# A planned first block and a squared relu: one shared port in the plan, a shift convolution summed in PSUM, and a relu that stays in its PSUM bank

## The chip, the cores and the metric

The kernel runs on one core of a Trainium2 chip. The metric is the device time of one execution in microseconds; the time given for a kernel is the median of its runs.

The engines carry the profile's names: PE multiplies matrices (PEld is its weight load), DVE and POOL work on vectors, ACT applies functions and copies, SP issues the DMAs. Each takes its own instructions strictly in order.

## The reference

Two layers, each a gated convolution (A) and a feed-forward net (B), on 2048 tokens of 1024 channels, in float32:

```python
def A(n, k, v, shift_k, ssm_k, ssm_D):       # n: layer norm of x
    k_shift = sum(k_pad[:, t:t + S] * shift_k[:, 3 - t] for t in range(4))
    kv = k_shift * v
    y = causal_long_convolution(kv, ssm_k) + kv * ssm_D    # 2048 taps, by FFT
    return n * y

def B(n, w1, b1, w2, b2):
    h = n @ w1 + b1                          # 1024 -> 3584
    return relu(h) ** 2 @ w2 + b2            # 3584 -> 1024

for layer in range(2):
    x = x + A(layernorm(x), k, v, shift_k, ssm_k, ssm_D)
    x = x + B(layernorm(x), w1, b1, w2, b2)
```

k, v and the convolution are the same in both layers, so the long convolution is worked out once and used twice.

## The kernel before

The tokens lie in four blocks of 512. A *unit* is one layer of one block. Eight units run in the order (0,0), (1,0), (0,1), (0,2), (1,1), (0,3), (1,2), (1,3) (layer, block). Units 0 to 4 are ordinary; units 5 to 7 (`WINO`) go through other code, which the change leaves alone.

**B of an ordinary unit.** The 28 groups `f` of 128 hidden features are taken one after the other. For one of them, m1 sums 8 slices of 128 channels into one PSUM bank. Each product is three matmuls (`mm3`, L327 to L329): operands are split into a rounded high part and a remainder, `xh`, `xl` and `whl`. So 24 matmuls of 512 columns fill a bank, in about 5.4 us, and m1's banks come from the ring `p1`, which has two. When a bank is full, `relu2` (L1395) turns it into the operands of the second product: with k = 0 relu, square and the rounded copy `rh` on ACT, with k = 1 the remainder `rl` on DVE. `lag.at(1, relu2, rs[c, a], 0)` (L1727) and `lag.at(2, relu2, rs[c, a], 1)` (L1728) put these one and two steps behind the matmuls. `give(o)` frees the bank; the next `f` but one is summed in it. `row()` is a tile of the ring `wr` in SBUF, which the weight rows use too. Weights reach SBUF in a first pass as w1 or w2 (`wr`), are split by ACT (L997) and DVE or POOL (L1005), and are written out as `wd`, from which later units load them.

**Beside B** the convolutions of blocks 1 to 3 are worked out: `fwd_x` and `fwd_g` make spectra, `prod_stream` multiplies them on POOL (L517), sums on DVE (L521) and adds and subtracts the results (`fin`, L527 and L528, POOL).

**The first block** has no B to run beside. `first_block` therefore lists tasks, and `Plan` gives them an order. A task has one or more pairs (engine, cost in ns), the tasks and buffers that it waits for, and a function that issues its instructions. `Plan.order` walks through time, always takes the ready task that can start first, on the engine where it would end first, and repeats this for 400 variations of the priorities; the variation with the earliest end is issued. For each of 8 groups `c` of 128 channels:

- `x_part`: the shift convolution (ACT L1102, three DVE instructions L1105 on an SBUF tile `fx`), the mult by v (L1108, POOL or DVE), transposes, two sets of matmuls, spectra `sx` (ACT, L1126 on DVE);
- `g_part`: the same for the kernel's spectra `sg` (L1165, L1167 on DVE), 8 additions of `ssm_D` to its first row (L1143), and the products `kd` that the next block needs;
- `prods`: for both halves `jj` three products of 256 or 512 elements (L1246, L1251), their sums (L1253), L1257, L1258, the butterfly L669/L670, the way back through PE, the gate with the layer norm (L1277), and the addition to x1 (L1285, POOL or DVE);
- behind `c` = 0 the layer norm's statistics and scaling (`ln_part`, L1187 to L1221).

At the end come `tails` (the second layer norm and its transposes, L1314, L1321, L1323) and eight weight steps (`weight`, L1334), the first matmuls of m1. `FILL` holds counts of idle transposes (L260) that are put into PE's waits.

Of the kernel before, what the change touches and what calls it, by code (L numbers as in the profile page):

```python
# [41 lines left out]
PLAN_TRIES = 400  # L42
NORM_0 = "VA"
# [6 lines left out]
FILL = (38, 45, 17)  # L50
# [45 lines left out]
class Plan:  # L96
# [37 lines left out]
    def order(self, rise, noise):  # L134
# [12 lines left out]
        while ready:  # L147
            best = None
            for i in ready:
                opts, _, _, bufs, lat, _ = self.tasks[i]  # L150
                t = at[i]
                ok = True
                for x in bufs:
                    if x not in made:
                        if x.after is not None and x.after not in made or x.prev is not None and left_users[x.prev]:
                            ok = False
                            break
                        if x.prev is not None and last[x.prev] > t:
# [11 lines left out]
            _, i, (e, c, st) = best  # L170
            _, _, _, bufs, lat, _ = self.tasks[i]
            free[e] = st + c
            end[i] = st + c + lat
# [13 lines left out]
    def run(self):  # L187
# [3 lines left out]
        for i in reversed(range(n)):  # L191
            opts, _, deps, _, lat, _ = self.tasks[i]
            self.height[i] += min(c for _, c in opts) + lat
# [5 lines left out]
        for k in range(PLAN_TRIES):  # L199
# [6 lines left out]
            got = self.order(rise, noise.tolist())  # L206
            if best is None or got[0] < best[0]:
                best = (*got, rise, noise)
# [13 lines left out]
def v2_cost(n):  # L222
    return 250 + 1.3 * n


def g_cost(n):
    return 200 + 2.45 * n
# [7 lines left out]
def tile_h3_mlp(ctx: ExitStack, tc: tile.TileContext, q, kT, vT, shk, ssmT, ssmD, w1, b1, w2, b2,  # L235
# [54 lines left out]
    V.memset(epst, EPS)  # L290

# [129 lines left out]
    def fwd_g(sb, c):  # L421
# [38 lines left out]
        V.tensor_add(oa[0], oa[1], k0)  # L460
# [50 lines left out]
    def prod_stream():  # L511
# [11 lines left out]
        def fin(st, sm, sb, g, k):  # L523
            s = sm.rearrange("p k j c -> p k (j c)")
            E = ENG[FIN[sb - 1]]
            if k == 0:
                E.tensor_add(s[:, 1], s[:, 0], s[:, 1])  # L527
                E.tensor_sub(s[:, 2], s[:, 0], s[:, 2])  # L528
# [135 lines left out]
    def flat(t, e):  # L664
        return t[:, e].rearrange("p (n c) -> p n c", c=CG)

# [376 lines left out]
    def first_block():  # L1043
# [8 lines left out]
        def sub(tag, n, off, shape, nm="xh"):  # L1052
# [3 lines left out]
            def make():  # L1056
                v = big[nm].t[:, off + i * size:off + i * size + size]
                return v if len(shape) == 2 else v.rearrange("p (a b) -> p a b", a=shape[1])
# [8 lines left out]
        with tc.tile_pool(name="pro", bufs=1) as pro:  # L1067
# [31 lines left out]

            def x_part(c, k4, v4):  # L1100
                ks = new(cv, "fx", 4, [P, T])
                pl.add([("A", a_cost(T))], lambda e: A.activation(  # L1102
                    ks.t, k4.t[:, 3:], AF.Copy, scale=shkt[:, c, 0:1]), [k4], [ks])
                for q_ in range(1, 4):
                    pl.add([("V", v2_cost(T))], lambda e, q_=q_: V.scalar_tensor_tensor(  # L1105
                        ks.t, k4.t[:, 3 - q_:T + 3 - q_], shkt[:, c, q_:q_ + 1], ks.t,
                        op0=OP.mult, op1=OP.add), [k4], [ks], lat=130)
                pl.add([("G", g_cost(T)), ("V", v2_cost(T))], lambda e: ENG[e].tensor_mul(  # L1108
                    ks.t, ks.t, v4.t), [v4], [ks])
# [5 lines left out]
                for r in range(2):  # L1115
# [8 lines left out]
                    pl.add([("A", a_cost(T))], lambda e, r=r, oi=oi: A.copy(spread(sp[r].t), sums(oi.t)), [oi], [sp[r]])  # L1124
                    if r:
                        pl.add([("V", v_cost(T))], lambda e, oi=oi: V.tensor_add(  # L1126
                            spread(sp[2].t), sums(oi.t), spread(sp[0].t)), [oi, sp[0]], [sp[2]])
                for i in range(3):
                    dma(lambda i=i: dview(XD[i], 0, c), lambda i=i: sp[i].t, [sp[i]])

            def g_load(c):
                raw = sub("lg", 2, 1560, [P, T])
                aux = sub("la", 2, 2584, [P, P])
# [3 lines left out]
                dma(lambda: aux.t[0:1], lambda: bass.AP(tensor=ssmD.tensor, offset=ssmD.offset + c * P,  # L1137
                                                   ap=[[0, 1], [1, P]]), w=[aux], cost=10)
                return raw, aux

            def g_part(c, raw, aux):
                keys = [(raw, 0), (raw, 1)]
                pl.add([("V", v_cost(P))], lambda e: V.tensor_add(raw.t[0:1, 0:P], raw.t[0:1, 0:P], aux.t[0:1]),  # L1143
                       [aux], [(raw, 0)])
# [5 lines left out]
                for r in range(2):  # L1150
# [11 lines left out]
                    if r == 0:  # L1162
                        pl.add([("A", a_cost(T))], lambda e, o=o: A.copy(spread(sp[0].t), sums(o.t)), [o], [sp[0]])
                    else:
                        pl.add([("V", v_cost(T))], lambda e, o=o: V.tensor_add(  # L1165
                            spread(sp[2].t), sums(o.t), spread(sp[0].t)), [o, sp[0]], [sp[2]])
                        pl.add([("V", v_cost(T))], lambda e, o=o: V.tensor_sub(  # L1167
                            spread(sp[1].t), sums(o.t), spread(sp[0].t)), [o, sp[0]], [sp[1]])
                o = bank("p1", 2, ps1)
                kd = new(cv, "fk", 2, [P, T])  # L1170

                def mmk(e):
                    for r in range(2):
                        for h in range(2):
                            s_ = slice(h * BL + P, h * BL + BL)
                            fmm(o.t[:, (2 * r + h) * P:(2 * r + h + 1) * P], base.t[:, 2 * h + r], raw.t[:, s_], True, True)
                pl.add([("PE", 900)], mmk, [*keys, *tabs], [o], rank=2e6)
                pl.add([("A", a_cost(T))], lambda e: A.copy(kd.t, o.t), [o], [kd])
                dma(lambda: KD[0][c], lambda: kd.t.rearrange("p (r n) -> p r n", r=2), [kd])
                for i in range(3):  # L1180
                    dma(lambda i=i: dview(GD[i], 0, c), lambda i=i: sp[i].t, [sp[i]])
# [8 lines left out]
            def moments(st, n):  # L1190
# [7 lines left out]
                pl.add([("V", 80)], lambda e: V.tensor_scalar(ve.t, mv.t[:, :, 1], EPS, None, op0=OP.add),  # L1198
                       al, [ve], lat=130)
                pl.add([("A", 190)], lambda e: A.activation(sd.t, mv.t[:, :, 1], AF.Sqrt, bias=epst), al, [sd])  # L1200
                pl.add([("V", 80)], lambda e: V.reciprocal(r.t, sd.t), [sd], [r], lat=130)
                pl.add([("V", 130)], lambda e: V.tensor_mul(t.t, r.t, r.t), [r], [t], lat=130)
                pl.add([("V", 130)], lambda e: V.tensor_mul(t.t, t.t, ve.t), [ve], [t], lat=130)
                pl.add([("V", 80)], lambda e: V.tensor_scalar(t.t, t.t, -0.5, 1.5, op0=OP.mult, op1=OP.add),
                       [], [t], lat=130)
                pl.add([("V", 80)], lambda e: V.tensor_mul(r.t, r.t, t.t), [t], [r], lat=130)
                pl.add([("V", 130)], lambda e: V.scalar_tensor_tensor(
# [3 lines left out]
            def norm(dst, x, keys, st, k, opts):  # L1211
                mv, r, nm = st["mv"], st["r"], st["nm"]
                for kh in range(2):
# [9 lines left out]
                    pl.add([(o, v_cost(512) if o == "V" else 720) for o in opts], go, [mv, r, nm, *keys[4 * kh:4 * kh + 4]],  # L1223
# [13 lines left out]

            def prods(c, jj):
                sm = new(cv, "sm", 2, [P, 3, 2, CU])
                xs, gs = spec["x", c], spec["g", c]  # L1240
                n = BL * (jj + 1)
                for ty, (xi, gi) in enumerate(PAIRS):
                    xt, gt = xs[xi], gs[gi]
                    opts = [("G", g_cost(n)), ("V", v2_cost(n) + 150)]
                    if jj == 0:
                        pl.add(opts, lambda e, ty=ty, xt=xt, gt=gt: ENG[e].tensor_mul(  # L1246
                            sm.t[:, ty], xt.t[:, :, 0], gt.t[:, :, 0]), [xt, gt], [(sm, ty)])
                        continue
                    pr = new(cv, "fx", 4, [P, T]) if c == KT - 1 else sub("ppr", 3, 512, [P, T], "xl")
                    pv = lambda t: t.rearrange("p (g b c) -> p g b c", g=2, b=BT)  # L1250
                    pl.add(opts, lambda e, xt=xt, gt=gt, pr=pr: ENG[e].tensor_mul(  # L1251
                        pv(pr.t), xt.t, gt.t[:, :, ::-1]), [xt, gt], [pr])
                    pl.add([("V", v2_cost(BL) + 100), ("G", g_cost(BL))], lambda e, ty=ty, pr=pr: ENG[e].tensor_add(  # L1253
                        sm.t[:, ty], pv(pr.t)[:, :, 0], pv(pr.t)[:, :, 1]), [pr], [(sm, ty)])
                two = [("G", g_cost(BL)), ("V", v2_cost(BL) + 100)]
                fl_ = lambda: sm.t.rearrange("p k g c -> p k (g c)")
                pl.add(two, lambda e: ENG[e].tensor_add(fl_()[:, 1], fl_()[:, 0], fl_()[:, 1]), [(sm, 0)], [(sm, 1)])  # L1257
                pl.add(two, lambda e: ENG[e].tensor_sub(fl_()[:, 2], fl_()[:, 0], fl_()[:, 2]), [(sm, 0)], [(sm, 2)])  # L1258
                z = {}
                pl.add([("V", 2 * v2_cost(BL) + 400), ("G", 2 * g_cost(BL))], lambda e: z.update(  # L1260
                    enumerate(butterfly(ENG[e], fl_()))), [], [(sm, 0), (sm, 1), (sm, 2)])
                o = bank("pt", 2, pst)

                def back(e):
                    if c == KT - 1 and jj == BT - 1:
                        fill(o.t, FILL[0])
                    for h in range(2):
                        oe = o.t[:, h * P:h * P + P]
                        for r in range(2):
                            fmm(oe, base.t[:, (5, 4, 3, 2)[2 * h + r]], z[h][:, r], r == 0, r == 1)  # L1270
                pl.add([("PE", 900)], back, [(sm, 0), (sm, 1), *tabs], [o])
                yo = new(cv, "fx", 4, [P, BL]) if c == KT - 1 else sub("yo", 2, 0, [P, BL], "xl")
                yn = new(cv, "fk", 2, [P, 2, P])
                sl = slice(c * P, (c + 1) * P)
                for e_ in range(2):
                    tt = 2 * jj + e_
                    pl.add([("V", v_cost(P))], lambda e, e_=e_, tt=tt: V.scalar_tensor_tensor(  # L1277
                        yn.t[:, e_], o.t[:, e_ * P:e_ * P + P], 1.0 / BL, ns[tt].t[:, sl],
                        op0=OP.mult, op1=OP.mult), [o, (ns[tt], c // 4)], [(yn, e_)])
                pl.add([("A", a_cost(256))], lambda e: A.activation(  # L1280
                    yo.t, o.t[:, 0:BL], AF.Copy, scale=1.0 / BL), [o], [yo])
                dma(lambda: YD[0][:, 2 * jj:2 * jj + 2, sl], lambda: yo.t.rearrange("p (e c) -> p e c", e=2), [yo], cost=400)
# [597 lines left out]
```

## Time and profile before

| | |
|---|---|
| median of 3 runs | 2758.64 us (2758.22 to 2763.38) |
| the profiled execution | 2754.0 us |
| its span, first to last instruction | 2752.2 us |
| mean granted TensorE clock | 0.995 |
| PE busy | 2696.8 us, 98% of the span |
| DVE, ACT, POOL busy | 2010.1, 1121.7, 922.5 us |
| first matmul of the first block; first weight matmul | 11.0 us; 140.45 us |

The page's busy times count overlapping work of several engines side by side, so they don't sum to the span. Since PE is 98% busy, an engine other than PE matters only where PE waits for it. The rows of a group give a line, engine and operation, the tiles as out<-in, their shapes and the count, then the busy time, the mean duration of one, and the engine's idle time just before with what ended it.

### The profile page before, as it was taken

What the parts mean: (1) busy time and instruction counts of PE and PEld (TensorE: products, weight loads), DVE (VectorE), ACT (ScalarE), POOL (GpSimd) and SP (SyncE); (2) the same over time, 40 slices, a digit from 0 to 9 for tenths busy, and PEclk for the clock granted to TensorE, in tenths of its full rate; (3) what the DMA queues carried; (4) which work ended last, traced back from release to release, by engine and by line L of the source; (5) the groups of instructions that cost most, each with busy time, mean ns of one, the idle gap of its engine ahead of it and who ended that gap; (6) DMA issues with size and microseconds to landing.
All of it is one profiled execution on the core that took longest, in us unless ns stands there. A gap on an engine that the chain in (4) does not pass through costs nothing.

```text
span 2752.2 us, 36801 instructions
## 1 busy us (share of the span) xinstructions
PE 2696.8 (98%) x12632; PEld 2238.5 (81%) x12632; DVE 2010.1 (73%) x3109; ACT 1121.7 (41%) x1935; POOL 922.5 (34%) x655
## 2 busy tenths in 40 slices
PE   7899999899999999999999999999999999999999
PEld 6888787788888888888888888888788788878887
DVE  8879888779888877788777665366687666664555
ACT  4254344343444333342234422254455444445443
POOL 6926665155542655326544454000100010001000
PEclk9999999999999999999999999999999999999999
DMA  8489988689989898788987877688888866676546
GB/s 261 164 295 334 306 294 288 238 281 376 345 290 316 306 335 298 257 318 294 344 280 250 314 277 266 226 290 304 297 289 294 281 228 210 230 258 208 176 165 203
DMA packets 378876, 755.86 MB, mean 275 GB/s; under 512 B 43704, under 2 KB 160576, under 8 KB 378688
## 3 DMA queue, kind: packets, MB, share of 16 engines
q1 hardware_dynamic: 378688, 753.50, 79.7%
q8 instruction: 100, 1.64, 0.2%
q14 instruction: 88, 0.72, 0.1%
HBM read 603.41 MB, written 149.95 MB: 274 GB/s over the span
## 4 chain that ended last, share of the span: by engine, by line
PE 84%; DVE 6%; DMA 5%; POOL 2%; issue 1%; ACT 1%; SPq 1%; DVEq 0%; ACTq 0%; POOLq 0%
PE p L327 26%; PE p L329 26%; PE p L328 26%; DMA whl<-wd_m 1%; DMA wr<-w 1%; PE pt L329 1%; PE pt L328 1%; PE pt L327 1%; DVE whl L1005 1%; DMA cg<-gd 1%; DMA whl<-wd_t 1%; PE p L1076 1%; PE pt L446 0%; PE pt L412 0%; PE pt L588 0%
## 5 line engine op out<-in xcount | busy, mean ns | idle before, releaser
L517 POOL TENSOR_TENSOR cp<-cx,cg 128x384 f32<-128x384 f32 (+5 forms) x288 | 540.9, 1891 | 587.7 <-DVE sm L521 383.6
L327 PE MATMUL p<-xh,whl 128*128 128x512 f32 (+1 forms) x1840 | 707.7, 385 | 2.0 <-DMA whl<-wd_m 1.9
L329 PE MATMUL p<-xh,whl 128*128 128x512 f32 (+1 forms) x1840 | 703.8, 382 | 0.6 <-POOL whl L1005 0.6
L328 PE MATMUL p<-xl,whl 128*128 128x512 f32 (+1 forms) x1840 | 703.6, 382 | 0.3 <-DVE xl L1323 0.3
L997 ACT CAST whl<-wr 128x512 fp32r<-128x512 f32 x638 | 384.4, 618 | 458.1 <-PE p L329 269.6
L1005 DVE TENSOR_TENSOR whl<-wr,whl 128x512 fp32r<-128x512 f32 x624 | 506.1, 831 | 72.9 <-ACT whl L997 66.9
L327 PE MATMUL p<-whl,rh 128*128 128x512 f32 x1372 | 547.4, 399 | 6.1 <-DMA whl<-wd_m 4.5
L328 PE MATMUL p<-whl,rh 128*128 128x512 f32 x1372 | 542.4, 395 | 4.2 <-DVE whl L1005 4.2
L329 PE MATMUL p<-whl,rl 128*128 128x512 f32 x1372 | 541.8, 395 | 0.0
L327 PEld LDWEIGHTS p<-xh,whl 128*128 128x128 f32 x1840 | 346.4, 188 | 71.0 <-DMA whl<-wd_m 2.0
L329 PEld LDWEIGHTS p<-xh,whl 128*128 128x128 f32 x1840 | 346.2, 188 | 68.9 <-POOL whl L1005 0.8
L328 PEld LDWEIGHTS p<-xl,whl 128*128 128x128 f32 x1840 | 346.2, 188 | 66.4 <-DVE xl L1323 0.5
L327 PEld LDWEIGHTS p<-whl,rh 128*128 128x128 f32 x1372 | 258.8, 189 | 67.3 <-DMA whl<-wd_m 7.7
L328 PEld LDWEIGHTS p<-whl,rh 128*128 128x128 f32 x1372 | 258.9, 189 | 63.7 <-DVE whl L1005 6.4
L329 PEld LDWEIGHTS p<-whl,rl 128*128 128x128 f32 x1372 | 258.7, 189 | 60.3
L1504 POOL TENSOR_TENSOR acc<-acc,px 128x512 f32<-128x512 f32 x18 | 23.1, 1323 | 774.7 <-DMA px<-b 774.7
L1407 DVE TENSOR_TENSOR rl<-wr,rh 128x512 fp32r<-128x512 f32 x140 | 142.2, 1016 | 179.9 <-ACT rh L1402 179.8
L521 DVE TENSOR_REDUCE sm<-cp 128x128 f32<-128x384 f32 (+5 forms) x288 | 249.0, 873 | 7.9 <-POOL cp L517 7.9
L1399 ACT ACTIVATE wr<-p,b1t 128x512 f32<-128x512 f32 x138 | 95.2, 690 | 371.6 <-PE p L329 369.8
L1468 DVE TENSOR_TENSOR rl<-wr,rh 128x256 fp32r<-128x256 f32 x84 | 49.4, 588 | 206.4 <-ACT rh L1463 206.3
L1527 DVE TENSOR_TENSOR acc<-p,acc 128x512 f32<-128x512 f32 x152 | 101.2, 687 | 89.2 <-PE p L329 88.6
L1460 ACT ACTIVATE wr<-p,b1t 128x512 f32<-128x512 f32 x84 | 57.9, 689 | 187.5 <-PE p L329 187.5
(270 smaller groups left out, 3437.1 us busy)
## 6 DMA issues: line engine op xcount, KB each, us to landing
whl<-wd_m SPq DMA_DIRECT2D x382, 512.0 KB, 5.6
wr<-w SPq DMA_DIRECT2D x494, 256.0 KB, 5.2
wr<-td SPq DMA_DIRECT2D x152, 256.0 KB, 4.4
wd_m<-whl SPq DMA_DIRECT2D x70, 512.0 KB, 6.5
cx<-xd SPq DMA_DIRECT2D x48, 512.0 KB, 5.4
cg<-gd SPq DMA_DIRECT2D x48, 512.0 KB, 6.9
gd<-fg SPq DMA_DIRECT2D x72, 256.0 KB, 6.2
cx<-xd SPq DMA_DIRECT2D x48, 384.0 KB, 6.0
```

Source lines behind the costliest of these rows:

```text
L327: PE.matmul(o, lh, rh, start=start, stop=False)
L328: PE.matmul(o, lh, rl, start=False, stop=False)
L329: PE.matmul(o, ll, rh, start=False, stop=stop)
L517: G.tensor_mul(pr.rearrange("p c i -> p i c"), xt[:, 0:j + 1], gt[:, j::-1])
L521: V.tensor_reduce(sm[:, ty, jj], st["pr"], axis=AX.X, op=OP.add)
L997: A.copy(t[:, 0], raws[n]["t"])
L1005: ENG[e[n % len(e)]].tensor_sub(t[:, 1], raws[n]["t"], t[:, 0].bitcast(F32))
L1399: A.activation(r, st["o"], AF.Relu, bias=b1t[:, st["f"]:st["f"] + 1])
L1407: V.tensor_sub(st["lo"], st["r"]["t"], st["hi"].bitcast(F32))
L1460: A.activation(r, st["o"], AF.Relu, bias=b1t[:, st["f"]:st["f"] + 1])
L1468: V.tensor_sub(st["lo"], r[:, 0:n], st["hi"].bitcast(F32))
L1527: V.tensor_add(accs[tt][:, d], o, accs[tt][:, d])
```

## The change

It has three parts.

1. **The plan.** A task's option may carry a third entry, which makes it hold the resource `port` while it runs, whichever of DVE and POOL has it; two such tasks are never planned at one time. The costs of DVE and POOL are lower, and a third of the tries each counts DVE's time once, one and a half times or twice in choosing an engine. `FILL` falls from (38, 45, 17) to (16, 45, 8).
2. **The first block.** The shift convolution is summed in a PSUM bank `kp`, and the mult by v reads it there, always on DVE. A channel group's three spectra lie in one tile, in such an order that one instruction multiplies two of the three kinds for both halves (`prods_both`, 1536 elements); one addition of 768, one product of 768, one addition of 1024 (`fold`, an operand read twice) and a butterfly of 512 follow. Pairs of groups share a PSUM bank and 256-wide gates. Of the sums of `g_part`, one kind is built from a negated ACT copy and a DVE subtraction. `ssm_D` is added once for all groups. The `kd` products move into `carry`, behind the last `g_part`, from two new loads of 1 MB. Elsewhere `fin` uses `fold` on POOL, and `fwd_g` makes one sum with the opposite sign.
3. **The relu.** `relu2` of the ordinary units works in place in m1's bank, and the bank is given back behind the DVE subtraction.

```diff
-                for e, c in opts:
-                    st = max(t, free.get(e, 0.0))
-                    if f is None or st + c < f:
-                        f, pick = st + c, (e, c, st)
+                for e, c, *own in opts:
+                    st = max(t, free.get(e, 0.0), free.get("port", 0.0) if own else 0.0)
+                    late = st + c + lean * c * (e == "V")
+                    if f is None or late < f:
+                        f, pick = late, (e, c, st, own)
...
 def v2_cost(n):
-    return 250 + 1.3 * n
+    return 140 + 1.055 * n
 def g_cost(n):
-    return 200 + 2.45 * n
+    return 170 + 2.19 * n
...
+    warm = const.tile([P, 1], F32)
+    A.activation(warm, epst, AF.Copy)
...
         V.scalar_tensor_tensor(oa[1], kk[0][:, 0:T], sgn[:, 0:1], oa[1], op0=OP.mult, op1=OP.add)
-        V.tensor_add(oa[0], oa[1], k0)
+        V.scalar_tensor_tensor(oa[0], oa[1], -1.0, k0, op0=OP.mult, op1=OP.subtract)
...
+    def fold(E, s):
+        E.tensor_add(s[:, 1:3], s[:, 1:3], s[:, 0:1].to_broadcast([P, 2, s.shape[2]]))
...
             def x_part(c, k4, v4):
+                kp = bank("p2", 4, ps2)
                 ks = new(cv, "fx", 4, [P, T])
                 pl.add([("A", a_cost(T))], lambda e: A.activation(
-                    ks.t, k4.t[:, 3:], AF.Copy, scale=shkt[:, c, 0:1]), [k4], [ks])
+                    kp.t, k4.t[:, 3:], AF.Copy, scale=shkt[:, c, 0:1]), [k4], [kp])
                 for q_ in range(1, 4):
-                    pl.add([("V", v2_cost(T))], lambda e, q_=q_: V.scalar_tensor_tensor(
-                        ks.t, k4.t[:, 3 - q_:T + 3 - q_], shkt[:, c, q_:q_ + 1], ks.t,
-                        op0=OP.mult, op1=OP.add), [k4], [ks], lat=130)
-                pl.add([("G", g_cost(T)), ("V", v2_cost(T))], lambda e: ENG[e].tensor_mul(
-                    ks.t, ks.t, v4.t), [v4], [ks])
+                    pl.add([("V", 750)], lambda e, q_=q_: V.scalar_tensor_tensor(
+                        kp.t, k4.t[:, 3 - q_:T + 3 - q_], shkt[:, c, q_:q_ + 1], kp.t,
+                        op0=OP.mult, op1=OP.add), [k4], [kp], lat=130)
+                pl.add([("V", v_cost(T))], lambda e: V.tensor_mul(ks.t, kp.t, v4.t), [v4, kp], [ks])
...
+            def carry(half):
+                rows = new(pro, "s" + "xg"[half], 4, [P, 2, T])
+                dma(lambda: rows.t, lambda: ssmT[BL:T, half * T:half * T + T].rearrange("(m e) c -> m e c", e=2),
+                    w=[rows], cost=1460)
+                for c in range(4 * half, 4 * half + 4):
+                    carry_part(c, rows, slice(c % 4 * P, c % 4 * P + P))
...
+            def prods_both(c):
...
+                pl.add([("G", g_cost(2 * n), 1), ("V", v2_cost(2 * n), 1)], lambda e: ENG[e].tensor_mul(
+                    slots(), both(xs), both(gs)[:, :, ::-1]), rd, [(sm, 0), (sm, 1)])
+                pl.add([("V", v2_cost(n), 1), ("G", g_cost(n), 1)], lambda e: ENG[e].tensor_add(
+                    at(1), at(0), at(1)), [(sm, 0)], [(sm, 1)])
+                pl.add([("G", g_cost(n), 1), ("V", v2_cost(n), 1)], lambda e: ENG[e].tensor_mul(
+                    at(0), both(xs)[:, :, 0], both(gs)[:, :, 0]), rd, [(sm, 0)])
+                pl.add([("G", g_cost(2 * T), 1), ("V", v2_cost(2 * T), 1)], lambda e: ENG[e].tensor_add(
+                    sm.t[:, :, 1:3], sm.t[:, :, 1:3], sm.t[:, :, 0:1].to_broadcast([P, BT, 2, 2 * CU])),
+                    [], [(sm, 0), (sm, 1)])
...
     def relu2(st, k):
+        o = st["o"]
         if k == 0:
-            st["r"] = row()
-            r = st["r"]["t"]
-            A.activation(r, st["o"], AF.Relu, bias=b1t[:, st["f"]:st["f"] + 1])
-            A.activation(r, r, AF.Square)
+            A.activation(o, o, AF.Relu, bias=b1t[:, st["f"]:st["f"] + 1])
+            A.activation(o, o, AF.Square)
             st["hi"] = ml.tile([P, T], F32R, name="rh", bufs=FC + 1)
-            A.copy(st["hi"], r)
-            if st["give"]:
-                give(st["o"])
+            A.copy(st["hi"], o)
         else:
             st["lo"] = ml.tile([P, T], F32R, name="rl", bufs=FC + 1)
-            V.tensor_sub(st["lo"], st["r"]["t"], st["hi"].bitcast(F32))
-            drop(st["r"])
+            V.tensor_sub(st["lo"], o, st["hi"].bitcast(F32))
+            if st["give"]:
+                give(o)
```

**DVE in the first block.** DVE's instructions before, from the middle of the first block (`sm` and `xl` hold products, `sx` and `sg` spectra, `fk` the gated result, `cg` and `cx` rows of x1, `pt` and `p1` PSUM banks):

```order
L1277 SCALAR_TENSOR_TENSOR fk_669<-pt_653,cp_327 128x128
L1285 TENSOR_TENSOR cg_177<-cg_177,fk_669 128x128
L1285 TENSOR_TENSOR cx_197<-cx_197,fk_669 128x128
L1165 TENSOR_TENSOR sg_695<-p1_630,sg_604 128x2x4x64
L1246 TENSOR_TENSOR sm_672<-sx_644,sg_604 128x256
L1246 TENSOR_TENSOR sm_672<-sx_641,sg_695 128x256
L1257 TENSOR_TENSOR sm_672<-sm_672 128x256
L1258 TENSOR_TENSOR sm_672<-sm_672 128x256
L1105 SCALAR_TENSOR_TENSOR fx_576<-xh_148,shkt_122,fx_576 128x512
L1143 TENSOR_TENSOR xh_148<-xh_148 1x128
```

And now, where a group's products are worked out (L1284 to L1290 are `prods_both`, L1125 and L1128 the convolution and its mult, L1354 and L1363 the gate and the addition to x1):

```order
L1128 TENSOR_TENSOR fx_569<-p2_542,fx_484 128x512
L1186 TENSOR_TENSOR sg_527<-sg_527,p1_552 128x2x4x64
L1284 TENSOR_TENSOR xl_277<-sx_544,sg_424 128x6x2x128
L1354 SCALAR_TENSOR_TENSOR fk_600<-pt_472,px_514 128x256
L1354 SCALAR_TENSOR_TENSOR fk_600<-pt_472,cp_498 128x256
L1188 TENSOR_TENSOR sg_527<-p1_552,sg_527 128x2x4x64
L1363 TENSOR_TENSOR cg_227<-cg_227,fk_600 128x256
L1288 TENSOR_TENSOR xl_277<-sx_544,sg_424 128x768
L1125 SCALAR_TENSOR_TENSOR p2_624<-xh_150,shkt_122,p2_624 128x512
L1290 TENSOR_TENSOR xl_277<-xl_277 128x2x512
```

Long products come in place of several short ones, the convolution's tile is a PSUM bank, and the mult by v stands on DVE in every group. Up to the first weight matmul DVE has 170 instructions in place of 214 and POOL 34 in place of 116 (without the constants set up at the start).

**PE in m1 of unit 0.** The last matmul into one bank and the first ones into the next, before (the brackets name the engines whose semaphores an instruction waits on):

```order
L329 MATMUL p1_2572<-xh_1286,whl_2463 128x512
L327 MATMUL p1_2637<-xh_1286,whl_2500 128x512 [waits Activation_49]
L328 MATMUL p1_2637<-xl_1292,whl_2500 128x512
L329 MATMUL p1_2637<-xh_1286,whl_2500 128x512 [waits DVE_49]
L327 MATMUL p1_2637<-xh_1286,whl_2500 128x512
```

and now:

```order
L336 MATMUL p1_2362<-xh_1084,whl_2250 128x512
L334 MATMUL p1_2429<-xh_1084,whl_2286 128x512 [waits DVE_49]
L335 MATMUL p1_2429<-xl_1089,whl_2286 128x512
L336 MATMUL p1_2429<-xh_1084,whl_2286 128x512
L334 MATMUL p1_2429<-xh_1084,whl_2286 128x512
```

The first matmul into a bank waited for ACT, whose relu was the last to read it; it now waits for DVE, whose subtraction is. The later wait on DVE before was for the split weight.

More of the change, by code (lines that the diff above doesn't have):

```diff
@@ L42 @@
 PLAN_TRIES = 400
+PLAN_LEAN = (0, 0.5, 1)
 NORM_0 = "VA"
@@ L1350, in first_block @@
             for c in range(KT):
-                for kind in "xg":
-                    spec[kind, c] = [new(pro, "s" + kind, 12, [P, 2, BT, CU]) for _ in range(3)]
+                for k in "xg":
+                    spec[k, c] = new(pro, "s" + k, 4, [P, 3, 2, BT, CU])
+            dma(lambda: first.t[0:KT, 0:P], lambda: ssmT[0].rearrange("(c d) -> c d", d=P), w=[(first, 0)], cost=10)
+            dma(lambda: first.t[0:KT, P:], lambda: ssmD.rearrange("(c d) -> c d", d=P), w=[(first, 1)], cost=10)
+            pl.add([("V", v_cost(P))], lambda e: V.tensor_add(first.t[0:KT, 0:P], first.t[0:KT, 0:P], first.t[0:KT, P:]),
+                   [(first, 1)], [(first, 0), first])
             gl = g_load(0)
```

195 lines of the change are left out of this document (122 added, 73 removed).

## The prediction

> **What bounds the kernel now.** I read the page's busy times first, then a table of stretches of the span, then groups and single rows of the stretches that the change touches.
>
> Busy time of the whole span, then four stretches (columns: start:end, length, busy PE, PEld, DVE, ACT, POOL with counts, granted clock, DMA share, GB/s), and the first weight matmul, which ends the first block's hold on PE:
>
> ```profile
> PE 2696.8 (98%) x12632; PEld 2238.5 (81%) x12632; DVE 2010.1 (73%) x3109; ACT 1121.7 (41%) x1935; POOL 922.5 (34%) x655
> ...
> 0.00:11.00 11.00, 0.00 (x0) 0.00 (x1) 4.31 (x7) 2.73 (x3) 2.41 (x7) 1.00 0.72 222
> 11.00:120.00 109.00, 100.06 (x573) 90.37 (x574) 100.88 (x167) 39.31 (x72) 91.61 (x92) 0.95 0.70 227
> 120.00:140.40 20.40, 15.66 (x108) 13.56 (x106) 16.34 (x41) 4.87 (x10) 13.24 (x18) 0.92 0.40 145
> 142.00:1830.00 1688.00, 1668.22 (x7960) 1392.37 (x7959) 1289.35 (x1798) 644.30 (x1141) 784.13 (x515) 1.00 0.86 297
> ...
> 140.45 0.39 PE L327 MATMUL p<-xh,whl 128*128 128x256 f32 x1
> ```
>
> From 142 to 1830 us, the five ordinary units, PE idles 20 us in 1688: any new wait there is paid in full. In the first block PE idles 24.7 of 140.4 us (11.0 + 8.9 + 4.7), while DVE is busy 121.5 (4.31 + 100.88 + 16.34) and POOL 107.3 (2.41 + 91.61 + 13.24). PE waits there for products of these two; the end of a row is what ended its idle time:
>
> ```profile
> L1076 PE MATMUL pt<-sm,yh 128*128 128x128 f32 x128 | 19.8, 296 | 9.8 <-POOL sm L669 5.6 <-DVE sm L669 2.2 <-POOL sm L670 1.0
> L412 PE MATMUL p<-ident,fx 128*128 128x128 f32 x32 | 6.5, 332 | 12.7 <-POOL fx L1108 11.4 <-DVE fx L1108 1.4
> ```
>
> So DVE and POOL together set the first block's end. Their groups up to 140.4 us (busy us, mean ns), then single rows with start and duration:
>
> ```profile
> L1105 DVE SCALAR_TENSOR_TENSOR fx<-xh,shkt,fx 128x512 f32<-128x512 f32 x24 | 22.7, 950 | 7.5 <-ACT fx L1102 7.5
> L1246 DVE TENSOR_TENSOR sm<-sx,sg 128x256 f32<-128x256 f32 x10 | 7.4, 751 | 0.8 <-PE pt L1076 0.8
> L1251 DVE TENSOR_TENSOR xl<-sx,sg 128x512 f32<-128x512 f32 x7 | 7.4, 1051 | 0.0
> L1258 DVE TENSOR_TENSOR sm<-sm 128x256 f32<-128x256 f32 x8 | 7.3, 911 | 1.9 <-POOL sm L1246 1.3 <-POOL sm L1253 0.6
> L1257 DVE TENSOR_TENSOR sm<-sm 128x256 f32<-128x256 f32 x8 | 6.8, 854 | 0.7 <-POOL sm L1253 0.7
> L1126 DVE TENSOR_TENSOR sx<-p,sx 128x512 f32<-128x512 f32 x8 | 5.4, 674 | 1.2 <-ACT sx L1124 1.2
> L1187 DVE BATCH_NORM_STATS2 st<-cg 128x6 f32<-128x512 f32 x8 | 5.4, 682 | 0.3 <-POOL cg L1285 0.3
> L1285 DVE TENSOR_TENSOR cx<-cx,fk 128x128 f32<-128x128 f32 x10 | 5.1, 513 | 0.0
> L1143 DVE TENSOR_TENSOR xh<-xh 1x128 f32<-1x128 f32 x8 | 4.8, 599 | 0.8 <-DMA xh<-ssmT 0.8
> L1277 DVE SCALAR_TENSOR_TENSOR fk<-pt,cp 128x128 f32<-128x128 f32 x24 | 6.4, 278 | 3.9 <-PE pt L1076 2.7 <-ACT fx L1280 1.2
> L1251 POOL TENSOR_TENSOR xl<-sx,sg 128x512 f32<-128x512 f32 x14 | 19.2, 1372 | 11.0 <-DVE ve L1198 9.8 <-DVE rs L1201 1.1
> ...
> 21.46 0.86 DVE L1246 TENSOR_TENSOR sm<-sx,sg 128x256 f32<-128x256 f32 x1
> 24.93 0.41 DVE L1246 TENSOR_TENSOR sm<-sx,sg 128x256 f32<-128x256 f32 x1
> 20.77 1.27 POOL L1251 TENSOR_TENSOR xl<-sx,sg 128x512 f32<-128x512 f32 x1 [9.82 <-DVE ve L1198]
> 24.26 0.73 POOL L1246 TENSOR_TENSOR sm<-sx,sg 128x256 f32<-128x256 f32 x1 [1.35 <-DVE sg L1167]
> ```
>
> One shape, two times: 0.41 us alone, 0.86 beside a POOL instruction. Rows with one operand in PSUM (L1126, 674 ns) are not stretched. The sizes give DVE about 0.14 us + 1.05 ns an element with both inputs in SBUF, POOL 0.17 us + 2.2 ns.
>
> **First block, term by term.** Rows up to the first weight matmul, at unstretched durations.
>
> DVE before, 97 us: 53 with both inputs in SBUF (24 L1105 at 0.74, 12 of 512 elements at 0.68, 38 of 256 at 0.41, 19 of 128 at 0.28, one subtraction of a weight, and the small layer norm rows) and 44 others. DVE after, 106 us: 44 and 62. The convolution goes to PSUM (24 at 0.75, as the nearest row, L457 below, has it) and its mult by v, 8 at 0.67, is no longer POOL's. Of the merged products DVE has 7 of 1536 elements (1.76 each, 12.3), 6 of 768 (0.95, 5.7), 6 folds of 1024 (1.22, 7.3) and 5 pairs of 512 (6.8); the 256-wide back parts (20, 6.9), half the adds (3.6), and the unchanged sums from PSUM and statistics make the rest. POOL falls from 90 us (116 instructions) to 43 (34). So DVE alone is 9 us longer, and with 44 fewer instructions, each of which overlaps the next by 0.07, another 3: **+12**.
>
> Stretch: DVE's durations in the block sum to 39 us more than unstretched (28 in the L1105, L1246, L1251, L1258, L1257, L1253, L1108 and L1285 groups, as 24 x 0.21 in the first; the rest in L1143 and two-column rows). That is near the 53 us of SBUF work times POOL's share of the time, 107.3/140.4 = 0.76, which is 40. After: 44 us x (43/124 = 0.35, some stretch of its own on top: 0.39) = 17: **-22**.
>
> Idle: DVE's 19 us hold 6.7 of ramp before 11 us, which stays but for about 1 us (the first mult is DVE's). The rest is mostly handoffs from POOL and ACT; with 34 of 116 POOL instructions left I let a third of it go: **-5**, the ramp's 1 us in it. PE's 12.7 us in front of L412 lie under these terms. Sum +12 - 22 - 5 = **-15**: the first weight matmul at about 125.5.
>
> Bounds: idle unchanged and stretch falling only as POOL's work (43/90): +12 - 20.5 = -8.5. The other end is PE: its 115.7 us of today, less 31 filling transposes of 0.14 (4.4), begun at 10 us, end at 121; where groups close up a little less, as each group's last matmul is counted in full. I put that end at 118, a gain of 22. The tail (layer norm, transposes, eight weight steps) keeps its instructions, and the 32 `kd` matmuls that `carry` puts there fill a PE that waits for DVE's statistics. `carry` adds 2 MB of loads and moves 2 MB of stores past the last spectra, in stretches where DMA is 0.70 and 0.40 busy: I cost it at nothing, or +3 if the first weights queue behind them on SP.
>
> [...]
>
> **The relu in PSUM.** ACT's three rows keep their number and read and write PSUM; ACT is 38% busy there (644 of 1688), so a tenth more or less of each costs nothing. The DVE subtraction reads PSUM; its price is bounded by a PSUM row and its own (minimum/median/maximum):
>
> ```profile
> L457 DVE SCALAR_TENSOR_TENSOR pt<-fk,sgn,pt x24: 741/747/751, 172.6 to 1411.0; 128x512 f32<-128x512 f32 x24
> ...
> L1407 DVE TENSOR_TENSOR rl<-wr,rh x140: 672/692/2902, 160.0 to 1820.2; 128x512 fp32r<-128x512 f32 x140
> L1407 DVE TENSOR_TENSOR rl<-wr,rh 128x512 fp32r<-128x512 f32 x140 | 142.2, 1016 | 179.9 <-ACT rh L1402 179.8
> ```
>
> Median 692, mean 1016: the stretch, 0.33 x 140 = 46 us of DVE, goes.
>
> [...]
>
> The price is the bank: only two `p1` banks serve m1, and `give` now comes after the subtraction. PE is in order, so behind its waiting matmul all matmuls queue, and then DVE's and ACT's work on them. I matched each subtraction with the next use of its bank: in today's trace 15 of 130 end after it, 37 us in all, first at 178.5, last at 1311.3. The first, the last and the three furthest, PE's next use above, the subtraction below:
>
> ```profile
> 178.54 0.39 PE L327 MATMUL p<-xh,whl 128*128 128x512 f32 x1
> 453.73 0.39 PE L327 MATMUL p<-xh,whl 128*128 128x512 f32 x1
> 634.35 0.39 PE L327 MATMUL p<-xh,whl 128*128 128x512 f32 x1
> 725.15 0.39 PE L327 MATMUL p<-xh,whl 128*128 128x512 f32 x1
> 1309.18 0.39 PE L327 MATMUL p<-xh,whl 128*128 128x512 f32 x1
> ...
> 178.51 0.69 DVE L1407 TENSOR_TENSOR rl<-wr,rh 128x512 fp32r<-128x512 f32 x1
> 457.76 0.82 DVE L1407 TENSOR_TENSOR rl<-wr,rh 128x512 fp32r<-128x512 f32 x1
> 638.35 0.68 DVE L1407 TENSOR_TENSOR rl<-wr,rh 128x512 fp32r<-128x512 f32 x1
> 731.01 0.68 DVE L1407 TENSOR_TENSOR rl<-wr,rh 128x512 fp32r<-128x512 f32 x1
> 1311.34 0.68 DVE L1407 TENSOR_TENSOR rl<-wr,rh 128x512 fp32r<-128x512 f32 x1
> ```
>
> Late by 0.7, 4.8, 4.7, 6.5 and 2.8: 19.5 us (the other ten mostly lie behind these in one backlog of DVE, which a stall of PE clears). [...] Against it stand waits of PE on DVE in the same stretch (total us, times, longest):
>
> ```profile
> PE pt L412 <- DVE fx L359: 5.0, 2, 4.8
> PE p L328 <- DVE whl L1005: 4.2, 3, 3.3
> PE pt L588 <- DVE fg L476: 1.4, 1, 1.4
> ```
>
> Of these 10.6 us a shorter DVE queue, and POOL's shorter fold (one instruction for two, 48 times), take perhaps a third: **-4**, between 0 and -8. The negated addition L460 and the early ACT table load are within a microsecond.
>
> **Sum.** The profiled execution took 2754.0 (span 2752.2), 4.6 below the median of 2758.64. 2754.0 - 15 + 9 - 4 = 2744, and +4.6 for the median: **2749** (2748.6). A measurement of this kernel can tell about 0.2%, 5.5 us, from no change.
>
> **Rivals.**
> - *Both gains whole*: port and handoffs stop counting, PE's own work ends the first block at 118, and DVE's shorter queue brings nearly every subtraction ahead of its bank's next use: 2758.6 - 22 + 2 - 6 = 2733. For it: the 11.4 us that L412 waits on POOL go wholly, and four of the five late rows lie behind instructions stretched by POOL. Against: DVE's 106 us barely fit. Chance 0.14.
> - *They cancel*: the first block gains 8.5, the lower bound, and the banks cost 12: 2758.6 - 8.5 + 12 - 4 = 2758. For it: DVE does more, not less, in the first block. Chance 0.22.
> - *The held bank* (slower): DVE's backlogs stay as long, and PE meets nearly all 37 us: 2758.6 - 15 + 35 - 2 = 2777. It decides from a bank wait of about 25 us, where gain and threshold are used up. For it: the five pairs above, and DVE 76% busy (1289 of 1688). Against: a stall lets DVE catch up, so that lateness in one backlog is paid once. Chance 0.17.
> - *The first block is no shorter*, so that the plan doesn't do what it says: DVE's 12 us more and longer POOL instructions, each holding up DVE's next, eat what stretch and idle give: 2758.6 + 0 + 9 - 2 = 2766. Against: 47 us less of POOL. Chance 0.08.
>
> The forecast itself has 0.39. Faster: 0.39 + 0.14 = 0.53; same 0.22; slower 0.17 + 0.08 = 0.25. Range: from 2731, just under both gains whole, to 2776, where about half of the held bank's case lies outside.
>
> **What would show it.** Right: the first weight matmul at 120 to 130, unstretched merged products, DVE rows of the relu near 0.69 throughout, and 2 to 20 us of PE waits on those rows, at conv stretches (around 455, 640, 730, 1310). Wrong: a first weight matmul after 135, or PE waits on the subtraction above 27 us, or such waits on ACT's rows.

## The result, and the profile after

The changed kernel takes 2758.56 us (median of 14 runs) where the one before, run beside it, takes 2757.89: a ratio of 1.000, with a 95% interval of 0.9992 to 1.0008. Nothing moved. The forecast of 2749 held a gain of 0.35%; the time lies within the range, in the case that the prediction called *they cancel*. The profiled execution has a span of 2756.1 us, 3.9 more than that of before.

The page's busy times, stretches of the span, and the first weight matmul of the changed kernel (columns as in the prediction):

```profile
PE 2694.2 (98%) x12601; PEld 2237.7 (81%) x12601; DVE 1935.9 (70%) x3068; ACT 1110.9 (40%) x1937; POOL 826.3 (30%) x531
...
0.00:11.00 11.00, 1.10 (x4) 0.72 (x4) 3.28 (x6) 2.28 (x4) 0.70 (x6) 1.00 0.59 175
11.00:105.00 94.00, 87.40 (x517) 79.59 (x518) 85.45 (x122) 38.55 (x66) 39.69 (x29) 1.00 0.81 257
105.00:123.40 18.40, 15.32 (x128) 14.07 (x128) 16.20 (x46) 9.52 (x19) 5.15 (x6) 1.00 0.79 287
142.00:1830.00 1688.00, 1653.87 (x7775) 1377.20 (x7774) 1217.34 (x1767) 617.64 (x1122) 747.78 (x465) 0.99 0.84 291
...
123.50 0.36 PE L334 MATMUL p<-xh,whl 128*128 128x256 f32 x1
```

The first weight matmul comes at 123.50, 16.95 us earlier. DVE has 72 us less between 142 and 1830, and POOL 96 us less over the span. Yet the end is where it was. The time went here, in the table of PE's waits from 142 to 1850 us (total us, times, longest):

```profile
PE p L334 <- DVE rl L1492: 19.0, 6, 5.0
PE pt L419 <- DVE fx L366: 6.1, 1, 6.1
PE p L335 <- DVE whl L1014: 4.9, 1, 4.9
```

L1492 is the subtraction of the relu. The six waits, each a first matmul of m1 with the idle time before it in brackets, and at the second of them DVE's queue up to the subtraction:

```profile
334.01 0.50 PE L334 MATMUL p<-xh,whl 128*128 128x512 f32 x1 [1.56 <-DVE rl L1492]
444.41 0.77 PE L334 MATMUL p<-xh,whl 128*128 128x512 f32 x1 [4.94 <-DVE rl L1492]
629.68 0.79 PE L334 MATMUL p<-xh,whl 128*128 128x512 f32 x1 [4.97 <-DVE rl L1492]
726.35 0.77 PE L334 MATMUL p<-xh,whl 128*128 128x512 f32 x1 [4.06 <-DVE rl L1492]
886.88 0.50 PE L334 MATMUL p<-xh,whl 128*128 128x512 f32 x1 [1.14 <-DVE rl L1492]
1317.13 0.50 PE L334 MATMUL p<-xh,whl 128*128 128x512 f32 x1 [2.31 <-DVE rl L1492]
...
438.31 3.56 DVE L364 SCALAR_TENSOR_TENSOR fx<-fx,shkt 128x512 f32<-128x512 f32 x3
441.91 1.10 DVE L366 TENSOR_TENSOR fx<-fx 128x512 f32<-128x512 f32 x1
442.93 0.41 DVE L482 TENSOR_TENSOR fg<-pt,fg 128x256 f32<-128x256 f32 x1
443.26 0.41 DVE L483 TENSOR_TENSOR fg<-pt,fg 128x256 f32<-128x256 f32 x1
443.59 0.68 DVE L1492 TENSOR_TENSOR rl<-p,rh 128x512 fp32r<-128x512 f32 x1
```

Work for a later block stands ahead of the subtraction, its shift convolution and sums for its kernel's spectrum: six instructions, over 5 us. In the trace before, PE did not wait for that subtraction; now it does, through the bank. Four of the six waits are at places that the prediction read off the old trace (454, 634, 725 and 1309 us there).

The waits of 4 to 5 us cost more than themselves here. Stretches behind the waits at 444 and 726 us (last three columns: granted clock, DMA share, GB/s):

```profile
444.40:447.00 2.60, 2.59 (x6) 2.12 (x7) 2.56 (x5) 0.00 (x0) 2.12 (x2) 0.50 0.00 0
447.00:450.00 3.00, 3.00 (x16) 2.54 (x16) 1.93 (x4) 0.00 (x0) 0.00 (x0) 0.79 0.67 219
450.00:453.00 3.00, 3.00 (x16) 2.48 (x16) 2.21 (x4) 0.49 (x2) 2.17 (x2) 1.00 0.74 216
726.30:729.00 2.70, 2.65 (x6) 2.15 (x7) 2.70 (x5) 0.00 (x0) 0.19 (x1) 0.50 0.83 299
729.00:732.00 3.00, 3.00 (x11) 2.38 (x10) 3.00 (x4) 0.00 (x0) 1.65 (x1) 0.57 0.01 5
732.00:735.00 3.00, 3.00 (x20) 2.67 (x19) 0.65 (x2) 0.60 (x1) 1.96 (x1) 1.00 0.00 0
```

PE works, but at a granted clock of 0.50 and then, over the next 3 us, at a mean of 0.79 or 0.57. As an estimate from these rows, 2.60 x 0.50 + 3.00 x 0.21 = 1.9 us are lost behind the first wait, and 2.70 x 0.50 + 3.00 x 0.43 = 2.6 behind the second.

### The profile page after: what moved, and what is told of

Same layout as the page of the kernel before. It is cut to its first block, busy times and chain, and to the rows that moved or that the text cites. A ratio compares the mean times of both kernels' runs of the same rounds, so it can differ in the third digit from the quotient of the medians.

```text
span 2756.1 us, 36563 instructions
## 1 busy us (share of the span) xinstructions
PE 2694.2 (98%) x12601; PEld 2237.7 (81%) x12601; DVE 1935.9 (70%) x3068; ACT 1110.9 (40%) x1937; POOL 826.3 (30%) x531
## 4 chain that ended last, share of the span: by engine, by line
PE 86%; DVE 6%; DMA 5%; issue 1%; ACT 1%; SPq 1%; POOL 0%; DVEq 0%; ACTq 0%; POOLq 0%
PE p L334 26%; PE p L335 26%; PE p L336 26%; PE p L1089 2%; DMA wr<-w 1%; PE pt L336 1%; PE pt L335 1%; PE pt L334 1%; DVE whl L1014 1%; DMA whl<-wd_m 1%; DMA wd_m<-whl 0%; PE pt L594 0%; PE p L788 0%; DVE sm L528 0%; DMA cg<-gd 0%
## 5 line engine op out<-in xcount | busy, mean ns | idle before, releaser
L524 POOL TENSOR_TENSOR cp<-cx,cg 128x384 f32<-128x384 f32 (+5 forms) x288 | 534.0, 1867 | 617.7 <-DVE sm L528 397.7
L1014 DVE TENSOR_TENSOR whl<-wr,whl 128x512 fp32r<-128x512 f32 x624 | 489.4, 805 | 76.9 <-ACT whl L1006 72.1
L1486 ACT ACTIVATE p<-p,b1t 128x512 f32<-128x512 f32 x138 | 91.7, 664 | 395.6 <-PE p L336 395.4
L1492 DVE TENSOR_TENSOR rl<-p,rh 128x512 fp32r<-128x512 f32 x138 | 94.9, 688 | 221.0 <-ACT rh L1489 220.8
L1546 ACT ACTIVATE wr<-p,b1t 128x512 f32<-128x512 f32 x84 | 58.0, 690 | 188.5 <-PE p L336 184.9
```

Source lines behind the costliest of these rows:

```text
L524: G.tensor_mul(pr.rearrange("p c i -> p i c"), xt[:, 0:j + 1], gt[:, j::-1])
L1014: ENG[e[n % len(e)]].tensor_sub(t[:, 1], raws[n]["t"], t[:, 0].bitcast(F32))
L1486: A.activation(o, o, AF.Relu, bias=b1t[:, st["f"]:st["f"] + 1])
L1492: V.tensor_sub(st["lo"], o, st["hi"].bitcast(F32))
L1546: A.activation(r, st["o"], AF.Relu, bias=b1t[:, st["f"]:st["f"] + 1])
```

## The experiments

Four questions were open: whether the two effects really cancel, whether the bank is the cause of the one, what part of the change makes the other, and what else the relu in PSUM brings. All times are medians beside the kernel before on the same chip, which took 2757.3 to 2757.6 in the three groups of runs.

**The first block alone, and the relu alone.** The first kernel is the changed one with the old relu2:

```diff
     def relu2(st, k):
-        o = st["o"]
         if k == 0:
-            A.activation(o, o, AF.Relu, bias=b1t[:, st["f"]:st["f"] + 1])
+            st["r"] = row()
+            A.activation(st["r"]["t"], st["o"], AF.Relu, bias=b1t[:, st["f"]:st["f"] + 1])
...
+            drop(st["r"])
```

> The changed kernel with relu2 as before the change (relu, square and remainder from a tile in SBUF, bank given back behind ACT), so the first block and the plan alone. Theory A (the first block gains its 17 us and the held bank takes them back): 2738 to 2746, first weight matmul at 123 to 124, no PE wait on the subtraction, PE waits after 142 us about as before the change (15 to 20 us). Theory B (the relu costs nothing net; what the first block gains is given back in the units by something else, such as the later stores and loads or DVE's other waits): 2754 to 2760.

2741.32 us, ratio 0.9941 (0.9929 to 0.9953): 16.0 us faster. The second is the kernel before with the new relu2:

> The kernel before with the new relu2 alone. Theory A: 2770 to 2782, that is 12 to 24 us slower, first weight matmul still at 140, six or so PE waits on the subtraction that sum to 15 to 22 us, and a lower granted clock for some microseconds behind each of the long ones. Theory B: 2754 to 2760, since DVE's shorter subtractions pay for the waits.

2776.69 us, ratio 1.0068 (1.0055 to 1.0080): 19.4 us slower. Its first weight matmul is at 140.37; its PE waits:

```profile
PE p L327 <- DVE rl L1404: 14.9, 5, 5.5
PE pt L412 <- DVE fx L359: 4.8, 1, 4.8
```

The waits sum to 14.9 us, just under what was expected. They belong to one execution, whose span is 16.6 us longer than that of the profile before, at a mean clock of 0.992 in place of 0.995; the median is 19.4 us longer. Theory B falls: the two parts of the change are worth -16 and +19 by themselves and about 0 together.

**More banks.** During m1 the four banks of `p2`, into which the second product is summed, stand idle. So three of seven sums can go there:

```diff
-                bank = ps1 if len(tts) == NT else ps2 if a < 4 else lambda: spare.pop(0)
+                bank = (ps2 if a in (2, 3, 4) else ps1) if len(tts) == NT else ps2 if a < 4 else lambda: spare.pop(0)
```

> The changed kernel, but the third, fourth and fifth of each seven m1 sums (full width) take their banks from the ring p2, which stands idle during m1, so that a bank is reused two sums later or more in place of the next but one. Theory A: no PE wait on the subtraction, 2732 to 2742, below the first-block-alone kernel by what the shorter subtractions bring (0 to 8 us). Rival (the stalls come from DVE's queue, and would only move to the next PE instruction that needs DVE): 2750 to 2758.

2734.99 us, ratio 0.9917 (0.9904 to 0.9930). No PE wait on the subtraction is left in the units:

```profile
PE pt L419 <- DVE fx L366: 4.6, 1, 4.6
PE p L1699 <- DVE wr L1690: 3.8, 1, 3.8
PE p L335 <- DVE whl L1014: 3.7, 2, 2.2
PE p L334 <- DMA whl<-wd_m: 1.9, 1, 1.9
```

This kernel is faster than the one before and the changed one, by 22 to 24 us. The rival, by which the stall would move on, is refuted: where the banks suffice, DVE's late subtraction is met by nobody. The spread banks with the old relu2 were not run; but no wait of PE in the units of the kernel before is on its relu, so there they have no such wait to take away. The same edit in the kernel before with the new relu2:

> The kernel before with the new relu2 and the banks spread over p1 and p2 in the same way: the relu in PSUM without its price. Theory A: 2748 to 2758 (0 to 8 us faster than before, what 46 us less of DVE bring). Rival (the subtraction from PSUM itself, or its waits, cost): 2762 or more.

2748.46 us, ratio 0.9965 (0.9953 to 0.9977): 8.9 us faster than before, at the upper end of the gain expected, and 28.2 faster than the relu alone without the spread banks. That difference is the price of the held bank; between the changed kernel and its spread twin it is 23.6 by the medians and 24.5 by the two traces (spans of 2756.1 and 2731.6). Of these 24.5, PE is idle 18.5 us longer (61.9 in place of 43.4) and busy 6.0 us longer (2694.2 in place of 2688.2). From the first relu on ACT to the last of unit 4 the changed kernel takes 27.1 us more: the six waits (19.0) and, estimated from the granted clock behind the four long ones, about 8 us. Against these 27.1, the changed kernel's first relu came 0.7 us earlier, and 1.9 us come back in units 5 to 7, whose code is the same.

**Issue the subtraction earlier.** If it is late because of what is queued ahead of it, it might go ahead of that:

```diff
-                lag.at(2, relu2, rs[c, a], 1)
+                lag.at(1, relu2, rs[c, a], 1)
```

> The changed kernel (banks from p1 alone), with DVE's subtraction issued one step behind the last matmul, with ACT's three instructions, in place of two. If the late subtractions are late because of what is queued ahead of them on DVE (theory A1), they move ahead of up to a step's work: PE waits on the subtraction fall from 19 to 3 to 12 us, 2742 to 2752. If the two banks are simply too few for relu, square, copy and subtraction in a row (theory A2), or DVE now waits for ACT in front of its other work, nothing is gained: 2754 to 2764.

2787.23 us, ratio 1.0114 (1.0096 to 1.0132): 30 us slower than before, outside both expectations. First come PE's waits in this kernel, then DVE's largest wait in it, and last the same wait of DVE in the changed kernel:

```profile
PE pt L419 <- DVE fx L366: 12.8, 5, 6.5
PE p L788 <- ACT wr L731: 9.8, 6, 3.3
PE pt L334 <- DVE fy L402: 6.9, 3, 4.1
PE p L334 <- DVE rl L1492: 3.0, 3, 1.4
...
DVE rl L1492 <- ACT rh L1489: 306.1, 110, 9.4
...
DVE rl L1492 <- ACT rh L1489: 223.3, 89, 9.4
```

The wait on the subtraction does fall, from 19.0 to 3.0. But DVE, in order, stands 83 us longer in front of it, waiting for ACT's copy, and everything behind it is late: the convolutions above all. Theory A1 had the queue right and left out what the moved instruction itself waits for. Theory A2 named this wait, and put its price 23 us too low.

**Parts of the first block.** Each of these has the spread banks, so they compare with 2734.99 us and a first weight matmul at 124.19; but the third is the kernel before with the new planner. First the old planner (costs of before, no port) on the new tasks:

> The kernel with spread banks, its first block planned with the costs of before and without the port (new instructions, old planner). It tells the plan's share in the 17 us of the first block. If the instructions make the gain (fewer and longer ones, convolution in PSUM): first weight matmul at 123 to 128, total 2735 to 2740. If the plan makes it: 133 to 140, total 2745 to 2752. I expect 127, total 2738.

2738.26 us. Then the convolution back on an SBUF tile:

> The kernel with spread banks, its shift convolution on an SBUF tile as before (24 additions with both inputs in SBUF, each holding the port in the plan; the mult by v on DVE or POOL). By the stretch term, 18 us of DVE work come back under the port while POOL is busy 0.37 of the time: 4 to 7 us later, first weight matmul at 128 to 131, total 2739 to 2743. If the merged products alone do it: 123 to 125, total 2735.

2742.94 us. Then the new planner on the old instructions:

> The kernel before with the new planner alone (port, new costs, the weighting of DVE) on its old instructions. If the plan is worth something by itself: first weight matmul at 130 to 137, total 2747 to 2754. If not: 139 to 143, total 2756 to 2761. I expect 136, since POOL gets fewer of the instructions but DVE has no room for many more.

2756.30 us, ratio 0.9997 (0.9988 to 1.0007). Then the old counts of idle transposes:

> The kernel with spread banks, with the idle transposes of before, FILL (38, 45, 17). If the 31 more of them lie in PE's waits: first weight matmul at 124 to 125, total 2734 to 2737. If PE's own work now sets the first block's end (the bound of 118 to 121 us in the prediction): 127 to 129, up to 4.4 us later, total 2738 to 2740. I expect the first.

2740.04 us. Their first weight matmuls, in this order:

```profile
125.79 0.39 PE L335 MATMUL p<-xh,whl 128*128 128x256 f32 x1 [0.24 <-ACT xh L1401]
...
129.18 0.38 PE L334 MATMUL p<-xh,whl 128*128 128x256 f32 x1
...
144.90 0.38 PE L332 MATMUL p<-xh,whl 128*128 128x256 f32 x1 [0.24 <-ACT xh L1326]
...
126.86 0.38 PE L334 MATMUL p<-xh,whl 128*128 128x256 f32 x1
```

So of the 16 us by which the first weight matmul moved, the convolution in PSUM makes 5.0, as expected. The planner's 1.6 is hardly more than the scatter between executions: five kernels that share the new first block (the changed one, the first block alone, the spread banks, the early subtraction, and the rows kept, below) have their first weight matmul at 123.50 to 124.97. The rest, about 10 us, is left for the merged instructions and what else changed with them, which were not tried alone. The planner on the old instructions makes the first block 4.4 us longer in its trace, against an expectation of 136. That execution's span is 5.6 us longer than the profile of before, so there the loss shows; the medians of the two kernels are the same, and one trace doesn't tell how typical the loss is.

With the old counts of idle transposes the kernel is 5.0 us longer by the median, and the first weight matmul comes 2.7 later, which was not expected. But most of the 2.7 is there before the first idle transpose runs, at 115.89. The sixteen matmuls of one spectrum and a stretch behind their start, with the old counts, and the same matmuls in the spread kernel:

```profile
105.17 3.22 PE L1089 MATMUL p<-sx,yh 128*128 128x128 f32 x16 [1.97 <-DMA sx<-ssmT]
106.00:109.00 3.00, 3.00 (x16) 3.00 (x15) 1.69 (x4) 1.10 (x2) 1.05 (x2) 0.50 0.80 286
...
104.64 2.02 PE L1089 MATMUL p<-sx,yh 128*128 128x128 f32 x16 [1.65 <-DMA sx<-ssmT]
```

The granted clock was 0.50 for these 3 us, the sixteen matmuls took 3.22 us where they take 2.02 in the spread kernel, and by the next matmuls of `sx` the kernel is 2.2 us late (110.44 in place of 108.28). The first 38 idle transposes take 4.31 us, 0.11 each where the prediction had 0.14. Whether they cost anything by themselves, and so whether PE's own work is near the end of 118 to 121 us that the prediction gave it, stays open.

**What the relu in PSUM brings beside its price.** In the spread kernel each relu takes a row of `wr` again, to be given back behind the subtraction:

```diff
+            st["r"] = row()
+            A.activation(st["r"]["t"][:, 0:1], b1t[:, 0:1], AF.Copy)
             A.activation(o, o, AF.Relu, bias=b1t[:, st["f"]:st["f"] + 1])
```

> The kernel with spread banks, where each relu still takes a row of the ring wr from the weights until its subtraction, as before the change (a one-column copy writes it, 140 small ACT instructions). It asks what the 6 to 9 us of relief are that came with the relu in PSUM. If it is the row that the weights get back: the relief goes, 2739 to 2743. If it is DVE's shorter subtraction and the port left free for POOL: 2734 to 2737.

2735.00 us, as without the rows. So it isn't that the weights have a row less to take in turn. The edit doesn't bring back all that the row did, though: the small copy is done before the relu starts, so a load into the row no longer waits for the subtraction. Before the change the loads (L989) did, eight times in the units:

```profile
SPq L989 <- DVE rl L1407: 8.7, 8, 2.3
```

What is left is these waits and DVE's shorter subtraction. Groups between 142 and 1830 us, POOL's products in the kernel before, then both in that kernel with the relu in PSUM and spread banks:

```profile
L517 POOL TENSOR_TENSOR cp<-cx,cg 128x384 f32<-128x384 f32 (+5 forms) x288 | 540.9, 1891 | 587.7 <-DVE sm L521 383.6 <-DMA cg<-gd 173.5 <-DMA cx<-xd 14.8
...
L1404 DVE TENSOR_TENSOR rl<-p,rh 128x512 fp32r<-128x512 f32 x138 | 94.8, 687 | 202.9 <-ACT rh L1401 202.5
L517 POOL TENSOR_TENSOR cp<-cx,cg 128x384 f32<-128x384 f32 (+5 forms) x288 | 532.1, 1859 | 607.0 <-DVE sm L521 373.2 <-DMA cg<-gd 204.7 <-DVE rl L1404 11.3
```

The subtraction's mean fell from 1016 to 687 ns, 46 us in all, and POOL's products from 1891 to 1859, 9 us. This is the likely source of the 6 to 9 us of relief; no run shows it by itself.

## Why the prediction held its range and missed its gain

- **First block, -15: right in sum.** Measured 16.95 in the profile of the changed kernel, and 16.0 in total time where the rest is undone. Inside the sum two terms were off and made up for each other. DVE's durations up to the first weight matmul sum to 115.5 us, where 106 were worked out unstretched: if those 106 are right, the stretch left is 9 us and not 17; the merged products of 1536 are hardly stretched at all (1755 ns in the median, 2086 at most). And DVE's idle time is 18.5 us (123.4 - 104.9 busy), where it was 18.9, not 5 less: its waits on POOL (2.9 us) went and those on PE fell from 3.5 to 0.6, but those on DMA rose from 0.8 to 7.1. DVE's largest groups up to 123.4 us, and PE's wait that was to go:

```profile
L1125 DVE SCALAR_TENSOR_TENSOR p<-xh,shkt,p 128x512 f32<-128x512 f32 x24 | 18.0, 751 | 3.9 <-ACT p L1122 3.5
L1284 DVE TENSOR_TENSOR xl<-sx,sg 128x1536 f32<-128x1536 f32 x7 | 12.7, 1810 | 0.7 <-PE pt L1089 0.6
L1290 DVE TENSOR_TENSOR xl<-xl 128x1024 f32<-128x1024 f32 x6 | 7.8, 1303 | 0.0
L1288 DVE TENSOR_TENSOR xl<-sx,sg 128x768 f32<-128x768 f32 x3 | 4.4, 1482 | 0.0
L419 PE MATMUL p<-ident,fx 128*128 128x128 f32 x32 | 5.8, 308 | 13.5 <-DVE fx L1128 13.5
```

  The prices taken from other rows were near: 751 ns for the addition in PSUM (0.75), 1810 and 1303 for the merged ones (1.76 and 1.22). But PE still waits 13.5 us in front of the transposes, where it waited 12.7: the releaser changed from POOL to DVE, and most of the wait is the ramp before the first matmul, 9.8 us now and 11.0 before. The waits that went are those on the butterfly: 9.5 us before, 0.6 now.
- **The stretch by shares of POOL's time.** By these shares 15 was worked out, and 17 was measured; no run tests the shares by themselves. That it counts where the convolution lies, its 5.0 us show: its additions took 732 to 1830 ns on the SBUF tile before (L1105, 752 in the median), and take 742 to 756 in PSUM (L1125, 754).
- **The held bank, +9: the step that failed.** The mechanism, its place and its raw sum were right: 19.0 us of waits against 19.5 read from the old trace. But +9 is about half of that, an estimate of the author that no run shows: the runs showed the 19.0 whole, and 24 to 28 us in all. To halve it DVE's backlogs would have had to shrink, and they did not: the convolution's additions, which stand in them, took 1148 ns in the mean where they had taken 1107, and 2792 at most where the median is 753, with POOL still busy beside them for 747.8 of 1688 us (784.1 before). And the forecast left out the clock, about 8 us in the units, though the trace before shows it behind the wait of 4.8 us that the prediction quotes. The additions before and now, and that stretch before (granted clock 0.56):

```profile
L357 DVE SCALAR_TENSOR_TENSOR fx<-fx,shkt 128x512 f32<-128x512 f32 x72 | 79.7, 1107 | 3.9 <-ACT fx L354 2.1
L364 DVE SCALAR_TENSOR_TENSOR fx<-fx,shkt 128x512 f32<-128x512 f32 x72 | 82.7, 1148 | 1.9
...
314.80:318.00 3.20, 3.13 (x10) 2.70 (x11) 3.20 (x6) 1.49 (x3) 0.93 (x1) 0.56 1.00 336
```

  The price was 24 to 28 us, between the 9 of the forecast and the 35 of the slower rival, and at the 25 us from which that rival was to decide.
- **Relief, -4: undersized.** 8.9 us in the kernel before, 6.3 in the changed one (2741.32 to 2734.99).
- **The subtraction from PSUM.** It takes 692 ns in the median, as it did from SBUF, and 693 at most, where the longest was 2902:

```profile
L1492 DVE TENSOR_TENSOR rl<-p,rh x138: 674/692/693, 142.7 to 1828.4; 128x512 fp32r<-128x512 f32 x138
```

Taken together, by the medians of the steps from the kernel before to the changed one: -16.0 for the first block, -6.3 for the relief and +23.6 for the bank make +1, where -15 - 4 + 9 = -10 was forecast. With the bank's price alone put right, at 24 to 28, the forecast would have been 5 to 9 us slower. That the kernel came out even, and not slower, is luck: the first block and the relief each brought a little more than forecast. And the range held because it was 45 us wide.

## What to carry to other kernels

A buffer that is read later is held longer. Match, in the trace at hand, the end of the new last reader with the next use of that buffer: the late ones are the price, to be taken whole unless something named takes them away, and what the granted clock showed behind waits as long comes on top, here an estimated 8 us on 19.0. When such a price is found, look for buffers that stand idle at that time before giving up what the longer hold brings; here one line on which bank to take turned 0 into 23 us. And an instruction moved ahead in an in-order queue brings its own wait along, here 83 us more of DVE waiting for ACT: ask what it waits for before asking what waits for it.

## What the runs showed that I had not expected

- Behind the three PE waits of 4 to 5 us the granted clock stood at 0.50 for 2.6 to 2.7 us or more, and over the next 3 us at a mean of 0.57 to 0.95: an estimated 1.5 to 2.6 us on top of each. Behind the wait of 1.14 us at 887 it stayed at 1.00, and so it did behind one of 3.3 us in the trace before, at 504. The mean clock of the changed kernel is 0.992, of its spread twin 0.997. The length of the wait alone doesn't sort them: behind the wait of 2.31 us at 1317, shorter than the one at 504, the clock stood at 0.50 from 1319 to 1322, and behind the one of 1.97 us at 105, with the old counts of idle transposes, from 106 to 109.
- The place of a matmul in one trace moves by a microsecond or two for reasons that the change didn't make: the same first block ended at 123.50 to 124.97 us in five kernels. A difference of that size between two traces is no finding.
- A subtraction issued one step earlier made DVE wait 83 us more for ACT and the kernel 29 us slower than the changed one, though it cut the wait that it was meant for from 19.0 to 3.0 us.
